# Moving the normalising passes of two layer norms from VectorE to GpSimd, with a new table of schedule settings

## The chip, the cores and the metric

The kernel runs on one core of a Trainium2 chip. A core has five engines that work side by side and wait for each other by semaphores: TensorE (PE, matmuls into the eight PSUM banks), VectorE (DVE), ScalarE (ACT), GpSimd (POOL) and SyncE (SP), which here issues nearly all DMAs. The metric is the device time of one execution in microseconds; of several runs the median is taken.

## The reference

From one input x of 2048 tokens by 512 features two branches are computed, and mixed by a gate of one number a token.

```python
def _layernorm(x, axis=-1, eps=1e-5):
    m = jnp.mean(x, axis=axis, keepdims=True)
    v = jnp.var(x, axis=axis, keepdims=True)
    return (x - m) / jnp.sqrt(v + eps)

# branch A: attention, 32 heads of 16
qkv = (x @ wqkv)                       # split into q, k, v by head
scores = einsum("bhqd,bhkd->bhqk", q, k) * (16 ** -0.5)
p = softmax(scores); o = einsum("bhqk,bhkd->bhqd", p, v)
a = o @ wo

# branch B: a mixer
h  = gelu(_layernorm(x) @ w1)          # 512 -> 512
hs = concat(four quarters of h, shifted by +1, -1, +2, -2 tokens) @ w2
x1 = x + hs
b  = x1 + gelu(_layernorm(x1) @ w3) @ w4   # 512 -> 1792 -> 512

g = sigmoid((x * gate_w).sum(-1))
out = g * a + (1 - g) * b
```

All inputs are bf16. Attention needs 32 x 2048 x 2048 exponentials; they are the largest piece of elementwise work.

## The kernel before

**Tiling.** Attention goes in 32 rounds: four chunks of 512 queries, four groups of eight heads, and the even or odd four heads of a group. A round has 64 score tiles, each 128 keys by 512 queries of one head: four heads on TensorE's four row groups, sixteen key tiles each. A score tile is one matmul (L1372, `qk_op`) and fills one PSUM bank. Altogether there are 2048.

**Two ways to the exponential.** Most score tiles go to ScalarE: `issue_act` (L1455) takes two or three tiles, and one exp instruction (L1467) turns their neighbouring banks into bf16 probabilities in SBUF (`prob`). For a three-tile instruction the knob `CAP3` has to allow it, for a two-tile one `CAP2` (L1783). The rest goes to VectorE: `issue_dve` (L1478) multiplies a score tile and adds an offset so that the result, rounded to a 16-bit integer, is the bit pattern of an approximate exponential (L1498). Two such tiles make a pair, and `close_pair` (L1518) derives three shifted copies of the pair by adding 32, 64 and 96 to the bits. A shift runs on VectorE (L1541) or on GpSimd (L1543); the knobs `GP2` and `GP3` set the share of either. The four versions together average the error out. A tile from ScalarE thus needs one value matmul (L1596, `take_pv`), a tile from VectorE four. Those write into one accumulator bank for a round, on TensorE's column groups.

**The end of a round.** `finish_round` (L1607) copies the accumulator to SBUF (L1617), sends the denominators through DRAM to be inverted and multiplied by the gate, and normalises on GpSimd (L1635); four small DMAs put the result into `oD`.

**The mixer.** The projections are matmuls of line L1002, cut into units of four matmuls on the four column groups; a few are done by rows (L1013). For a layer norm, `stats` (L1172 on) computes mean and variance of a 128-token tile on VectorE. `normalise` (L1180) handles a chunk of four tiles: variance plus epsilon (L1183) and its power of -0.5 (L1185) on GpSimd, minus mean times that (L1187) on VectorE, and then, for each tile, one pass over 128x512 (L1194) that multiplies by the one and adds the other. Its output is one of two `xn` buffers, which a DMA writes to DRAM (L1198) and frees; four transposing DMAs (L1204) read the chunk back into an `xnT` buffer, on which the matmuls with w1 or w3 depend. There are four chunks and two layer norms, so 32 passes. GELU runs over large blocks on ScalarE (L1214), with a table load before and another after (L1216).

**What sets the order.** The kernel's program is written out by a planner in Python while it is built (class `Sim`). Each engine has a list of jobs with a dependency list, a priority and an assumed duration (`hold`); `try_engine` (L330) lets a free engine take the ready job of the lowest priority number. TensorE's work is chosen by `pe_pick` (L1770): first score tiles for ScalarE and VectorE, then, in the time that it believes is left, units of projections and value matmuls. What it emits is the fixed order of each engine's instructions. Priorities and limits are knobs in a namespace `K`, from `BASE`, and a table `STEPS` overwrites some of them each time another `SEG = 8` score tiles have been issued:

```python
        if sim.tiles // SEG != stage[0]:
            for n in range(stage[0] + 1, sim.tiles // SEG + 1):
                K.__dict__.update(STEPS.get(n, {}))
```

Among them are `P1_PRIO` and `S_PRIO` (priorities of L1498 and L1541), `DVE_WAIT`, `DVE_STOP` and `DVE_ALONE` (how many tiles go to VectorE and when), `AHEAD` (how far score tiles may run into the next round), `MAXU` (most passes in one TensorE burst), `GATE` and `ROT`.

**The shared port.** `dve(..., port=True)` and every `gp(...)` job are ordered with one another: while one of them is believed to run, the planner starts no other, and each GpSimd instruction of that kind gets a wait for the last VectorE instruction of that kind before it (`in_port_order`, L315).

Of the kernel before, what the change touches and what calls it, by code (L numbers as in the profile page):

```python
# [452 lines left out]
def kernel(  # L453
# [14 lines left out]
    nc = tc.nc  # L468
# [66 lines left out]
        4: dict(P1_PRIO=0.136),  # L535
        5: dict(E_PRIO=0.1),
        6: dict(MAXU=3),
        7: dict(GP2=1, B_LOW=5),
        8: dict(E_PRIO=0.25, JOIN=1),
        9: dict(GP2=0.655),  # L540
        10: dict(GP2=1),
        11: dict(DVE_ALONE=-158),
        12: dict(LIMD=4),
        13: dict(AFIRST=0),
        14: dict(AFIRST=1),
        16: dict(DVE_STOP_L=16, PV_IDLE=0.117, PRESS=26),
        17: dict(IDLE_NS=864, B_LOW=8, ROT=0),
        18: dict(S_PRIO=0.38),
        19: dict(GP3=0.9),
        21: dict(GP3=0.8),  # L550
        22: dict(URG_L=18, PRESS=18),
        24: dict(GP3=0.9, URG_L=12, PRESS=26),
        25: dict(GP3=0.8, DVE_STOP=13, URG_L=18, PRESS=18),
        26: dict(AHEAD2=24, DUE_SH=32, GATE=3),
        27: dict(ROT=1),
        28: dict(SL0=-75, LIMA=2),
        29: dict(MAXG=2),
        30: dict(GP3=0.9, DUE_SH=-9),
        31: dict(GP3=0.8, DUE_SH=32),
        32: dict(GP3=0.967),  # L560
        33: dict(GP3=0.9, DUE_SH=-9),
        34: dict(PV_FULL=0.86, DUE_SH=16),
        35: dict(DVE_ALONE=2, ROT=0),
        36: dict(IDLE_NS=537, ROT=2, GATE=2),
        37: dict(P1_PRIO=0.55, ROWM=3),
        38: dict(SL1=-75, PV_FULL=0.813),
        39: dict(GP3=1, MAXG=1),
        40: dict(ROT=1),
        41: dict(S_PRIO=0.625, SL0=0, B_LOW=3, HOLE=2),
        42: dict(P1_PRIO=0.743, S_PRIO=0.3, GP3=0.8, DVE_STOP=4, DVE_STOP_L=14, URG=8, URG_L=12, DVE_ALONE=362, SL0=-75,  # L570
            IDLE_NS=374, AHEAD=12, PV_FULL=0.97, PV_IDLE=0.731, HOLE=3, MAXG=2, E_PRIO=2, AFIRST=2, ROWM=99, LIMA=4,
            JOIN=0),
        43: dict(ROT=2, AGE=6000),
        44: dict(MAXU=2, AGE=3000),
        45: dict(DVE_STOP_L=16, CAP2=5),
        46: dict(DVE_STOP_L=14, MAXU=3, CAP2=6, AGE=6000),
        47: dict(DVE_STOP=13, IDLE_NS=459, LIMA=3),
        48: dict(E_PRIO=0.4),
        49: dict(AT_SH=118),
        50: dict(ROT=3, ACC2=1),  # L580
        51: dict(GP3=1),
        52: dict(DVE_ALONE=-158, GATE=3, AGE=3000),
        53: dict(PV_FULL=0.813),
        54: dict(P1_PRIO=0.312, AHEAD=24),
        55: dict(BRES=2, MAXG=1),
        56: dict(URG=3, URG_L=18, SL1=-150, ROT=0),
        57: dict(URG_L=12, SL1=60, AGE=20000),
        58: dict(ROT=1),
        59: dict(SL1=130, B_LOW=2, PV_FULL=0.947),
        61: dict(LIMA=2),  # L590
        62: dict(SL1=-150),
        63: dict(P1_PRIO=0.55, DVE_STOP=8, URG=8, SL0=0, SL1=0, IDLE_NS=700, B_LOW=8, BRES=0, AHEAD=16, PV_FULL=0.86,
            PV_IDLE=0.117, ROT=0, DUE_SH=32, MAXG=2, GATE=2, E_PRIO=2, ACC2=0, LIMA=4),
        64: dict(URG=2, IDLE_NS=864, ROWM=3),
        65: dict(ROT=1),
        67: dict(E_PRIO=0.1),
        68: dict(URG=8, IDLE_NS=700, PV_FULL=0.947, CAP2=4, E_PRIO=2, ROWM=99, ACC2=1),
        69: dict(P1_PRIO=0.312),
        70: dict(LIMA=2),
        71: dict(GP3=0.8),  # L600
        74: dict(AHEAD=24, ROWM=3, LIMA=4),
        75: dict(URG=11),
        76: dict(DVE_WAIT=2),
        77: dict(URG=8, ROT=0, AGE=12000),
        79: dict(URG=11, DVE_WAIT=3, ROT=2, AGE=20000),
        80: dict(DVE_WAIT=2, ROT=1),
        81: dict(GP3=0.967),
        82: dict(URG=8),
        83: dict(P1_PRIO=0.279),
        84: dict(P1_PRIO=0.136, S_PRIO=0.38, GP3=1, URG=11, IDLE_NS=537, DVE_WAIT=3, AHEAD=3, PV_IDLE=0.5, ROT=0,  # L610
            AT_SH=34, CAP2=6, AGE=12000, ROWM=99, LIMA=3),
        85: dict(ACC2=0),
        86: dict(DVE_STOP_L=7, ROT=1),
        87: dict(DVE_STOP_L=14, ROT=0, ACC2=1),
        88: dict(AHEAD=9),
        89: dict(MAXU=9),
        90: dict(AGE=6000),
        91: dict(LIMA=2),
        93: dict(ROT=2),
        94: dict(ROT=0),  # L620
        95: dict(URG=2),
        96: dict(MAXU=2, JOIN=1),
        97: dict(MAXU=9, JOIN=0),
        98: dict(P1_PRIO=0.55, DVE_WAIT=4, PV_FULL=0.86),
        99: dict(LIMA=4),
        100: dict(URG=8, AT_SH=118),
# [1399 lines left out]
```

## Time and profile before

| | |
|---|---|
| Median of 3 runs | 744.62 us (744.61 to 744.85) |
| The profiled execution, in all | 744.89 us |
| Its span, first to last instruction | 742.9 us |
| TensorE clock granted | 1.000 |
| TensorE (PE) busy | 732.1 us, 99% |
| ScalarE (ACT) busy | 729.8 us, 98% |
| VectorE (DVE) busy | 678.8 us, 91% |
| GpSimd (POOL) busy | 479.0 us, 64% |
| DMA traffic | 34.60 MB, 47 GB/s on average |

The profile is of one execution. Busy time is time in which an engine has at least one instruction under way; two that overlap are counted once, but the mean duration of a group counts each in full, so 744 exps of 1.1 us fit into 685 us. Rows of groups read: line, engine, operation, output and input, shapes, count; then busy time in us and the mean in ns; then the idle time of the engine before these instructions and what ended it. Rows in order of time begin with start and duration in us. Rows of waits name who waited for whom, the time in all, how often, and the longest. PEld is the loading of weights into TensorE.

### The profile page before, as it was taken

Reading aid. Unit: us, or ns where it says so; the run is one execution under the profiler, and the core shown is the slowest. Engines: PE = TensorE matmul, PEld = TensorE weight load, DVE = VectorE, ACT = ScalarE, POOL = GpSimd, SP = SyncE. Lnnn points to the kernel's source line nnn. Section 1 sums busy time; section 2 is a strip of 40 time slices with the busy share of each in tenths; the row PEclk is TensorE's granted clock in tenths of the full one; section 3 lists DMA queues with packets and bytes.
Section 4 is the critical chain, followed back from the end, with each engine's and each line's share of the span. In section 5 each row is a group of like instructions: output and inputs, shape, how many; then the busy total and the mean of one; then the engine's idle time right before and its main releaser. Section 6 shows DMA issues by size and latency. Waiting matters only on the chain.

```text
span 742.9 us, 23801 instructions
## 1 busy us (share of the span) xinstructions
PE 732.1 (99%) x9550; PEld 212.8 (29%) x9550; DVE 678.8 (91%) x1407; ACT 729.8 (98%) x767; POOL 479.0 (64%) x478
## 2 busy tenths in 40 slices
PE   9999999999999999999999999999999999999997
PEld 5443232232222222222322222222222232222222
DVE  5899999999999999898998988999999997999995
ACT  7999999999999999999999999999999999999996
POOL 2247657788776757678557776667777767564441
PEclk9999999999999999999999999999999999999999
DMA  9520234022102132124100110002100000011001
GB/s 199 157 58 5 67 85 91 20 48 67 56 20 63 42 78 55 50 80 95 31 18 14 30 46 15 26 22 48 24 24 18 22 20 20 21 28 24 22 11 43
DMA packets 67094, 34.60 MB, mean 47 GB/s; under 512 B 46748, under 2 KB 62380, under 8 KB 66984
## 3 DMA queue, kind: packets, MB, share of 16 engines
q1 hardware_dynamic: 66040, 32.56, 17.6%
q8 instruction: 74, 1.21, 0.7%
q10 hardware_dynamic: 944, 0.52, 0.2%
q14 instruction: 36, 0.29, 0.1%
HBM read 17.40 MB, written 6.81 MB: 33 GB/s over the span
## 4 chain that ended last, share of the span: by engine, by line
PE 82%; ACT 13%; DVE 3%; issue 2%; ACTq 0%; DVEq 0%
PE banks L1596 29%; PE banks L1372 28%; PE banks L1002 24%; ACT prob L1467 10%; ACT hB L1214 2%; DVE prob L1541 1%; DVE prob L1498 1%; PE banks L981 0%; PE banks L1033 0%; ACT L1214 0%; ACT hT L1214 0%; ACT L1216 0%; PE banks L1127 0%; DVE accsb L1973 0%; DVE accsb L1976 0%
## 5 line engine op out<-in xcount | busy, mean ns | idle before, releaser
L1467 ACT ACTIVATE prob<-banks 128x1024 bf16<-128x1024 f32 (+1 forms) x744 | 685.3, 1146 | 1.1 <-PE banks L1002 0.8
L1543 POOL TENSOR_SCALAR prob<-prob 128x1024 uint16<-128x1024 uint16 x416 | 426.9, 1048 | 218.8 <-DVE prob L1541 97.0
L1498 DVE TENSOR_SCALAR prob<-banks 128x512 uint16<-128x512 f32 x553 | 367.1, 684 | 37.1 <-PE banks L1372 31.9
L1596 PE MATMUL banks<-prob,V 128*17 128x512 bf16 (+1 forms) x3713 | 313.5, 381 | 0.3
L1372 PE MATMUL banks<-q,kT 32*128 32x512 bf16 x2048 | 277.8, 384 | 3.6 <-ACT prob L1467 1.6
L1541 DVE TENSOR_SCALAR prob<-prob 128x1024 uint16<-128x1024 uint16 x418 | 158.4, 431 | 2.9 <-PE banks L1596 0.9
L1372 PEld LDWEIGHTS <-kT 32*128 32x128 bf16 x2048 | 69.9, 91 | 305.6 <-ACT prob L1467 282.0
L1596 PEld LDWEIGHTS <-V 128*17 128x17 bf16 (+1 forms) x3713 | 70.3, 88 | 116.3 <-issue 97.1
L1002 PE MATMUL banks<-xnT,w 128*32 128x512 bf16 x1152 | 96.5, 383 | 0.0
L1002 PE MATMUL banks<-w,hT 128*32 128x512 bf16 x692 | 59.7, 383 | 0.0
L1002 PEld LDWEIGHTS <-w 128*32 128x32 bf16 x1936 | 42.6, 95 | 50.3 <-issue 29.3
L1635 POOL TENSOR_TENSOR oT<-accsb,bcs 128x512 bf16<-128x512 f32 x31 | 39.5, 1275 | 26.1 <-DVE prob L1541 15.8
L1002 PE MATMUL banks<-w,w 128*32 128x256 bf16 (+1 forms) x784 | 41.0, 308 | 0.5 <-DVE prob L1498 0.4
L1002 PE MATMUL banks<-w,hB 128*32 128x512 bf16 x448 | 36.2, 382 | 0.4 <-ACT hB L1214 0.4
L1013 PE MATMUL banks<-wo,oD 32*128 32x512 bf16 x64 | 24.2, 384 | 0.0
L1617 DVE COPY accsb<-banks 128x512 f32<-128x512 f32 x31 | 21.2, 683 | 1.9 <-PE banks L1596 1.4
L1174 DVE BATCH_NORM_STATS2 st<-x_sb 128x6 f32<-128x512 bf16 x32 | 21.4, 678 | 0.0
L1002 PEld LDWEIGHTS <-hT 128*32 128x32 bf16 x692 | 14.7, 95 | 20.5 <-issue 14.2
L1268 DVE CAST hB<-banks 128x512 bf16<-128x512 f32 x28 | 18.9, 682 | 1.0 <-PE banks L1002 0.9
L1268 DVE CAST hT<-banks 128x512 bf16<-128x512 f32 x28 | 19.1, 682 | 0.7 <-PE banks L1002 0.5
L1002 PE MATMUL banks<-wo,oD 128*32 128x512 bf16 x176 | 19.5, 383 | 0.0
L1214 ACT ACTIVATE hT<-hT 128x7168 bf16<-128x7168 bf16 (+1 forms) x3 | 19.4, 6454 | 0.0
(94 smaller groups left out, 258.9 us busy)
## 6 DMA issues: line engine op xcount, KB each, us to landing
bcs<-rr SPq DMA_DIRECT2D x124, 64.0 KB, 2.0
xn_dram<-xn SPq DMA_DIRECT2D x32, 128.0 KB, 1.9
w<-in_B_w_dram SPq DMA_DIRECT2D x5, 512.0 KB
oD<-oT SPq DMA_DIRECT2D x124, 16.0 KB, 1.8
w<-in_B_w_dram SPq DMA_DIRECT2D x4, 448.0 KB
out_dram<-ot SPq DMA_DIRECT2D x14, 128.0 KB, 1.7
x_sb<-in_A_x_dram SPq DMA_DIRECT2D x3, 512.0 KB
w<-in_A_wqkv_dram SPq DMA_DIRECT2D x2, 256.0 KB
```

The costliest lines, as they stand in the source:

```text
L1002: units.append([Op("col", j, lambda j=j, lf=lf, rf=rf, n0=n0, n1=n1, st=st, sp=sp: nc.tensor.matmul(get()[32 * j:32 * j + 32, n0:n1], lhsT ...
L1013: o = Op("row", i, lambda: nc.tensor.matmul(get(), lhsT=lf(0, P)[rows], rhs=rf()[rows], start=False, stop=True, tile_position=(32 * i, 0), ...
L1174: a = dve(600, deps, lambda: nc.vector.bn_stats(out=sb.slot[:], in_=x_sb[:, t, :]), prio=6, at=at, acq=[sb])
L1214: g = nc.scalar.activation(out=ap, in_=ap, func=ACT.Gelu_apprx_tanh)
L1268: pre.append(evac(g, PSUM_NS, lambda ps, m=m: nc.vector.tensor_copy(out=h2()[:, m, :], in_=ps[:])))
L1372: o = Op("row", i, lambda: nc.tensor.matmul(dst(), lhsT=kT[G][32 * i:32 * i + 32, kt * P:(kt + 1) * P], rhs=qbuf[G, c].slot[32 * i:32 * i ...
L1467: job = act(hold, ops, lambda: nc.scalar.activation(out=prob[:, pb.cut(), :].bitcast(BF16), in_=unit()[:, rb.cut(), :], func=ACT.Exp, scal ...
L1498: return nc.vector.tensor_scalar(out=prob[:, b0.cut() if w == 2 else b0.bufs[h0].slot, :], in0=unit()[:, rb.cut() if w == 2 else rb.bufs[0 ...
L1541: return nc.vector.tensor_scalar(out=cut(k), in0=cut(0), scalar1=float(SHIFT * k), scalar2=None, op0=ALU.add)
L1543: return nc.gpsimd.tensor_scalar(out=cut(k), in0=cut(0 if both else 2), scalar1=1.0, scalar2=float(SHIFT * (k if both else 1)), op0=ALU.mu ...
L1596: return nc.tensor.matmul(one(accs[r])[32 * i:32 * i + n, :], lhsT=lhs(n), rhs=rhs(), start=st and not edge, stop=True, tile_position=(0, ...
L1635: n = gp(1250, d3, lambda: nc.gpsimd.tensor_tensor(out=ob.slot[:], in0=ab.slot[:], in1=bb.slot[:], op=ALU.mult), acq=[ob], frees=[ab, bb], ...
```

## The change

The pass of L1194 is created as a GpSimd job in place of a VectorE job, with an assumed duration of 592 ns for 323, and so on the GpSimd queue and in its port order:

```diff
             xb = Buf("xn", 1)
-            g = dve(323, [m], lambda t=t, xb=xb: nc.vector.tensor_scalar(
+            g = gp(592, [m], lambda t=t, xb=xb: nc.gpsimd.tensor_scalar(
                 out=xb.slot[:], in0=x_sb[:, t, :], scalar1=rs[which][:, t:t + 1], scalar2=nm[which][:, t:t + 1],
-                op0=ALU.mult, op1=ALU.add), prio=0.35, acq=[xb], port=True)
+                op0=ALU.mult, op1=ALU.add), prio=0.35, acq=[xb])
             last.append(g)
```

All of `STEPS` is replaced by another table, of which this is the beginning; the code that reads it is the same, and so is `BASE`:

```diff
     STEPS = {
-        0: dict(S_PRIO=0.3, DVE_STOP_L=7, SL0=0, IDLE_NS=374, AHEAD=16, AT_SH=69, AFIRST=1, AGE=20000),
-        1: dict(SL0=45, B_LOW=5, DVE_WAIT=1, AHEAD=9),
-        2: dict(AHEAD=7, MAXU=4, ACC2=1),
-        3: dict(SL0=0, B_LOW=3, DVE_WAIT=3, AHEAD=16, MAXU=9, ACC2=0),
...
+        0: dict(GP2=1, DVE_STOP=13, URG_L=18, SL0=60, MAXU=2, E_PRIO=0.25),
+        1: dict(P1_PRIO=0.55, URG_L=12, HOLE=0),
+        2: dict(AGE=20000),
+        3: dict(GP3=1, AT_SH=118),
+        4: dict(P1_PRIO=0.414, GP3=0.967, DVE_ALONE=-158, SL0=45, DVE_WAIT=2, AHEAD=16, AHEAD2=24, PV_FULL=0.86, MAXU=9,
+            AT_SH=34, HOLE=7, CAP3=5, GATE=4, E_PRIO=2, AGE=9000, ROWM=3),
...
```

Because the order is planned as a whole, a different table gives a different order on every engine, and other numbers of two-tile and three-tile exps, of score tiles on VectorE and of shifts on GpSimd. Counted in the built programs:

| instructions | before | after |
|---|---|---|
| exps over two tiles, three tiles, one tile (L1467) | 739, 5, 0 | 687, 42, 1 |
| score tiles on ScalarE, on VectorE | 1493, 555 | 1501, 547 |
| shifts of a pair on VectorE (L1541), on GpSimd (L1543) | 415, 416 | 444, 375 |
| normalising passes on VectorE, on GpSimd (L1194) | 32, 0 | 0, 32 |
| value matmuls (L1596) | 3713 | 3689 |
| DMAs issued by SyncE | equal | equal |

More of the change, by code (lines that the diff above doesn't have):

```diff
@@ L542 @@
[L542 to L568, printed above, removed]
@@ L614 @@
[L614 to L626, printed above, removed]
-        101: dict(P1_PRIO=0.414, AT_SH=0, ACC2=0),
-        102: dict(AFIRST=1),
```

387 lines of the change are left out of this document (194 added, 193 removed).

## The prediction

> **What bounds the kernel now.** I read the engine totals first, then ScalarE's own instructions in order of time, then the waits, and last the chain of work, which shows how TensorE and ScalarE hand over to each other.
>
> ```profile
> span 742.9 us, 23801 instructions
> PE 732.1 (99%) x9550; PEld 212.8 (29%) x9550; DVE 678.8 (91%) x1407; ACT 729.8 (98%) x767; POOL 479.0 (64%) x478
> 8.74 50.69 ACT L1467 ACTIVATE prob<-banks 128x1024 bf16<-128x1024 f32 x55
> ...
> 59.41 93.79 ACT L1467 ACTIVATE prob<-banks 128x1024 bf16<-128x1024 f32 x102
> 153.22 1.28 ACT L1214 ACT_TABLE_LOAD   x1
> ...
> 162.97 137.76 ACT L1467 ACTIVATE prob<-banks 128x1024 bf16<-128x1024 f32 x150
> 301.52 43.19 ACT L1467 ACTIVATE prob<-banks 128x1024 bf16<-128x1024 f32 x47 [0.79 <-PE banks L1002]
> 344.73 1.28 ACT L1214 ACT_TABLE_LOAD   x1
> ...
> 359.68 243.05 ACT L1467 ACTIVATE prob<-banks 128x1024 bf16<-128x1024 f32 x263
> 602.75 1.28 ACT L1214 ACT_TABLE_LOAD   x1
> ...
> 617.71 116.97 ACT L1467 ACTIVATE prob<-banks 128x1024 bf16<-128x1024 f32 x127
> 738.35 0.69 ACT L1992 ACTIVATE ot<-banks,omg 128x512 bf16<-128x512 f32 x1 [3.67 <-PE banks L1989]
> ```
>
> ScalarE runs without a gap from 8.74 us to 734.7 us, but for 0.79 us before 301.52. Its six stretches of softmax exponentials (L1467, "exps" below) are 50.69+93.79+137.76+43.19+243.05+116.97 = 685.45 us for 744 instructions. Between them lie three GELU blocks: 153.22 to 162.97 (9.75 us), 344.73 to 359.68 (14.95) and 602.75 to 617.71 (14.96). Ahead are 8.74 us, behind 742.9 - 734.68 = 8.2 us. That makes up the span. TensorE's 99% is not the same kind of number: who waits for whom must be asked.
>
> ```profile
> PEld L1372 <- ACT prob L1467: 282.0, 641, 1.0
> POOL prob L1543 <- DVE prob L1541: 97.0, 53, 8.6
> DVE prob L1498 <- PE banks L1372: 31.9, 89, 1.3
> 303.54 0.45 PE banks L1372 x4
> 303.98 0.54 PE banks L1596 x8
> 304.52 0.33 PE banks L1372 x3
> 304.85 0.59 PE banks L1596 x8
> ...
> 307.57 0.76 PE banks L1002 x12
> 308.33 0.32 PE banks L1372 x3
> ```
>
> The weight loads of the score matmuls (L1372) waited 641 times for an exp: TensorE gets its banks back from ScalarE. The chain shows the beat: a burst of scores 0.33 us, then eight other matmuls, which are two passes over the four column groups, 0.54 us: 0.87 us. Twelve, three passes, take 0.76 us, so a pass is 0.22 us and a change between bursts 0.54 - 2x0.22 = 0.10 us. VectorE has 64 us idle in the span and GpSimd 264 us.
>
> What one exp costs in the beat is read from the first and last starts in two stretches:
>
> ```profile
> L1467 ACT ACTIVATE prob<-banks x24: 1020/1162/1277, 118.3 to 139.1; 128x1024 bf16<-128x1024 f32 x24
> L1467 ACT ACTIVATE prob<-banks x7: 1168/1582/1657, 427.5 to 434.2; 128x1536 bf16<-128x1536 f32 x4, 128x1024 bf16<-128x1024 f32 x3
> L1467 ACT ACTIVATE prob<-banks 128x1024 bf16<-128x1024 f32 x739 | 679.8, 1143 | 1.1 <-PE banks L1002 0.8
> L1467 ACT ACTIVATE prob<-banks 128x1536 bf16<-128x1536 f32 x5 | 8.0, 1593 | 0.0
> ```
>
> The first row: 23 steps in 20.8 us, 0.904 us for an exp over two score tiles. The second: three wide and three narrow exps in 6.7 us, 2.233 a pair, so an exp over three tiles takes 1.329, and a tile more costs 0.425. (The durations of 1143 and 1593 ns overlap; they are not the pitch.) All 744 at these prices are 739x0.904 + 5x1.329 = 674.7 us. The stretches with their hole are 686.2; the six last exps drain some 0.24 us each, 1.4 together; the rest, 10.1 us, is waiting in small pieces. So ScalarE is the bound, with 10 us of slack in it at most.
>
> **The change, part by part.** Counts of the changed kernel are from its built program; durations are of the rows quoted.
>
> *The exps.* The new table of settings makes 687 two-tile exps of 739, 42 three-tile ones of 5, and one over a single tile (priced 0.904 - 0.425 = 0.479). That is 1501 score tiles on ScalarE for 1493, in 730 instructions for 744. The sum: -52x0.904 + 37x1.329 + 0.479 = -47.0 + 49.2 + 0.5 = **+2.6 us**, all on the path. Eight tiles are 8x0.425 = 3.4 us, and fourteen instructions saved give back 14x(0.904 - 0.850) = 0.8.
>
> The Trainium skill, "ScalarE: Activation LUTs", section "What ACT_TABLE_LOAD costs", gives another price for the step: 186 ns + 0.833 ns an element, less about 93 ns of overlap. By it the steps would be estimated at 0.946 and 1.373 us and the sum at +2.1; the trace's 0.904 is lower than that, and I keep the trace's.
>
> *The normalising passes.*
>
> ```profile
> L1194 DVE TENSOR_SCALAR xn<-x_sb,rs,nm 128x512 bf16<-128x512 bf16 x32 | 13.1, 433 | 1.3 <-DMA xn_dram<-xn 1.2
> L1543 POOL TENSOR_SCALAR prob<-prob 128x1024 uint16<-128x1024 uint16 x416 | 426.9, 1048 | 218.8 <-DVE prob L1541 97.0 <-PE banks L1596 38.2 <-PE banks L1372 24.8
> L1635 POOL TENSOR_TENSOR oT<-accsb,bcs 128x512 bf16<-128x512 f32 x31 | 39.5, 1275 | 26.1 <-DVE prob L1541 15.8 <-DMA bcs<-rr 3.6 <-DVE xn L1194 2.7
> L1708 POOL MEMSET oD<- 128x512 bf16 x1 | 0.5, 525 | 0.0
> L1498 DVE TENSOR_SCALAR prob<-banks 128x512 uint16<-128x512 f32 x553 | 367.1, 684 | 37.1 <-PE banks L1372 31.9 <-issue 0.2 <-PE banks L1596 0.2
> L1541 DVE TENSOR_SCALAR prob<-prob 128x1024 uint16<-128x1024 uint16 x418 | 158.4, 431 | 2.9 <-PE banks L1596 0.9 <-ACT prob L1467 0.6
> ```
>
> 32 passes of 0.433 us leave VectorE, 13.9 us. On GpSimd no such pass is shown: the 512-wide memset is 0.525 us, the two-input 512-wide product 1.275, the same kind of operation at double width 1.048. It lies nearest to half of the last plus its fixed part; I take 0.62, so 20 us, with ends of 17 and 41. GpSimd at the same time does 375 shifts (L1543) for 416: -41x1.048 = -43. It ends between 453 and 477 us busy, under the 479 it has: covered, and 0 on the path. Without this cover a chunk of four passes would cost up to 4x1.275 = 5.1 us once it is on the path.
>
> *VectorE's other work.* 547 score tiles (L1498) for 555: 547 single ones for 551, and none of two double ones, about -4x0.684 - 2x1.22 = -5.2. The shifts (L1541) rise by 29, +29x0.431 = +12.5. With the passes gone: -6.6 of 679 us. VectorE is not the bound, so 0.
>
> *TensorE.* Counting four matmuls on different column or row groups as one pass: column passes 1834 to 1819.5, row passes 709 to 724, changes between bursts 1404 to 1412: +0.5x0.22 + 8x0.10 = +0.9 us, on an estimated 2543x0.22 + 1404x0.10 = 700 us. ScalarE's exps and GELU blocks are 674.7 + 39.7 = 714. So TensorE has some 2% to spare, and +0.9 is hidden as long as single bursts are. A burst of three passes beside a two-tile exp (0.33 + 0.76 against 0.904) is over by 0.18: those rise from 98 to 109, at most +2.0. Bursts of four rise from 8 to 29, but 20 of the 29 stand beside a three-tile exp with 1.329 us of cover. I take 0 and keep +2.0 as the end.
>
> *Queues.* SP issues as many DMAs as before, the 32 writes of xn and 32 transposing reads among them, with the writes in another place:
>
> ```profile
> xn_dram<-xn SPq DMA_DIRECT2D x32, 128.0 KB, 1.9
> xnT<-xn_dram SPq DMA_TRANSPOSE x32, 2.7
> 300.66 0.41 DVE L1194 TENSOR_SCALAR xn<-x_sb,rs,nm 128x512 bf16<-128x512 bf16 x1 [0.42 <-DMA xn_dram<-xn]
> ```
>
> There are two xn buffers. The third pass of a chunk waits until the first's write has landed (1.9 us after issue); on VectorE that held up everything behind it for 0.42 us here. On GpSimd the same wait would hold shifts, and with them the value matmuls of their tiles, which are late next; its 97 us of waiting for VectorE's shifts alone are larger than 16 waits of 1.9. In the programs the last transposing read of a chunk precedes its first matmul by at least 11 exps, 10 us, where it was 6 before, against 2.7 us to landing. So 0.
>
> Head and tail: the same instructions lie before the first exp and, but for the width of the last one, behind it: 0.
>
> Sum: +2.6. The profiled execution took 744.89 us in all, its span 742.9; 744.89 + 2.6 = 747.5. It lies 0.27 above the median of 744.62, so I expect a median of **747.3 us**, +0.35%. About 0.2%, 1.5 us, is what a measurement of this kernel can tell from no change.
>
> **Rivals.**
>
> *The waits shrink: faster.* VectorE has 6.6 us less to do and its hold-ups by L1194 are gone, three-tile exps give bursts of four passes their cover, and the 10.1 us of small waits go to half: 747.3 - 5 = 742.3. The point from which it decides is 2.6 + 1.5 = 4.1 us of 10.1. For it speaks that the largest single hole (0.79 us before 301.52, behind an L1002 burst) comes right where VectorE stood 0.42 us at an xn pass. Against it: the other holes are too short for the waits to list, VectorE itself waits 31.9 us for scores, so relieving it need not bring scores sooner, and three-pass bursts beside two-tile exps become more. 0.12.
>
> *Gain and loss cancel:* the waits give back between 1.2 and 4: within 1.5 us of 744.6. The order was made anew throughout, and I have no row for its waits. 0.14.
>
> *GpSimd comes onto the path.* If a pass there is as slow as the product (1.275), or waits in line behind a shift (1.048), xn is written later and the first matmuls of a chunk hold up TensorE, which works in order. At the one hole of 0.79 us shown for each of eight chunks: +6.3, 753.6; at two or three chunks 749 to 750. The distances of 10 us and more speak against it. Within it, three-pass bursts that overshoot add up to 2.0: 749.3. Together 0.14.
>
> The Trainium skill speaks for that rival: "GPSIMD Engine Reference", section "4.1 Engine selection", sends elementwise work on a tile to VectorE and calls GpSimd about twice as slow with two inputs, though near line rate with one. An estimate by the 2.6 cycles an element of its section 3.1 is 1.1 us a pass; that lies inside the ends above, and no run here shows it yet.
>
> *The move doesn't do what it says:* the passes do leave VectorE in the built program, so no chance is kept for that.
>
> **How the numbers follow.** The forecast, 746.2 to 749.0, has 0.60; GpSimd or TensorE adding more 0.14; no measurable change 0.14; faster 0.12. So slower 0.74, same 0.14, faster 0.12. The range runs from 744.2, which leaves out the rival of shrunken waits but takes in most of the cancelling case, to 750.4, which is 747.3 + 2.0 and another hole of 0.79 with 0.3 to spare; about 2 in 10 stay outside.
>
> **What would show it.** Steps over two tiles of 0.904 and over three of 1.33; ScalarE without gaps from 8.7 us on, its stretches adding up to 688 or 689; xn on GpSimd at 0.6 us with GpSimd's busy time near 456 and VectorE's near 672; the rows of waits of L1002 for xnT empty. It is wrong if the stretches of exps are 685 or shorter (small waits gone), if xn passes come out above 1 us with holes on ScalarE before L1002 bursts, or if the tail behind the last exp is no longer 8.2 us.

## The result, and the profile after

The changed kernel takes 748.81 us (median; 748.21 to 750.36) and the kernel before, run beside it, 744.74 us (744.61 to 745.33). The ratio is 1.0050, with a 95% interval of 1.0031 to 1.0069: 4.1 us more, where 747.3 us and +2.6 were forecast. The profiled execution took 749.05 us in all, its span 747.2. In the profile of the changed kernel each line from the one of the exps on has a number 39 lower than before: exps L1428, score tiles on VectorE L1459, shifts L1502 (VectorE) and L1504 (GpSimd), scores L1333, value matmuls L1557, projections L963, passes L1155.

The page of the changed kernel (its span and engine totals), and ScalarE's instructions in order of time (start, duration, then what they are; in brackets the idle time ahead and who ended it):

```profile
span 747.2 us, 23772 instructions
PE 733.6 (98%) x9534; PEld 214.5 (29%) x9534; DVE 685.4 (92%) x1398; ACT 733.0 (98%) x753; POOL 463.3 (62%) x469
8.47 59.57 ACT L1428 ACTIVATE prob<-banks 128x1024 bf16<-128x1024 f32 x55
...
67.91 16.41 ACT L1428 ACTIVATE prob<-banks 128x1024 bf16<-128x1024 f32 x14
84.90 30.58 ACT L1428 ACTIVATE prob<-banks 128x1024 bf16<-128x1024 f32 x27 [0.58 <-PE banks L1333]
115.69 45.52 ACT L1428 ACTIVATE prob<-banks 128x1536 bf16<-128x1536 f32 x49 [0.21 <-PE banks L1333]
...
170.97 104.14 ACT L1428 ACTIVATE prob<-banks 128x1024 bf16<-128x1024 f32 x113
275.71 69.77 ACT L1428 ACTIVATE prob<-banks 128x1024 bf16<-128x1024 f32 x76 [0.59 <-POOL prob L1504]
...
360.45 232.91 ACT L1428 ACTIVATE prob<-banks 128x1024 bf16<-128x1024 f32 x254
...
608.33 115.76 ACT L1428 ACTIVATE prob<-banks 128x1024 bf16<-128x1024 f32 x126
724.32 14.35 ACT L1428 ACTIVATE prob<-banks 128x1024 bf16<-128x1024 f32 x16 [0.24 <-ACT prob L1428]
```

The nine stretches add up to 689.01 us for 730 exps, against 685.45 for 744. At the prices of the prediction (0.904, 1.329, 0.479) the exps of the changed kernel are 677.3 us against 674.7: +2.6. Four holes, all in brackets above, make 0.58 + 0.21 + 0.59 + 0.24 = 1.62 us, against one of 0.79. Stretches and holes, less the price and less the 1.4 us that the ends drain, are what ScalarE waited inside: 11.9 us, against 10.1. So the trace splits the 4.3 us by which the span grew into **+2.6 of more exponentials, +1.8 of more waiting**, 0.3 less ahead of the first exp (8.47 for 8.74) and 0.3 more behind the last (747.2 - 738.67 = 8.5 for 8.2), within rounding.

The three GELU blocks cut the span into four parts. In each, the time from the first exp to the last, less its exps at their prices and with the drains left in, is what ScalarE waited there: 2.5, 3.7, 3.6 and 1.7 us before, and 3.8, 3.7, 3.3 and 2.4 us after. So the added waiting lies ahead of the first GELU block, where half of the passes and all three-tile exps stand, and behind the last, where no pass stands; between the first and the second, where the other half of the passes stands, there is none.

Two of the four holes lie at normalising passes. Around the first, the trace of the changed kernel in order of time:

```profile
81.81 0.77 POOL L1155 TENSOR_SCALAR xn<-x_sb,rs,nm 128x512 bf16<-128x512 bf16 x1 [1.18 <-DMA xn_dram<-xn]
82.55 2.22 POOL L1504 TENSOR_SCALAR prob<-prob 128x1024 uint16<-128x1024 uint16 x2
82.82 2.23 DVE L1502 TENSOR_SCALAR prob<-prob 128x1024 uint16<-128x1024 uint16 x2
83.65 0.40 PE L1557 MATMUL banks<-prob,V 128*17 128x512 bf16 x4 [0.99 <-POOL prob L1504]
```

GpSimd stands 1.18 us at a pass, until the DMA that writes an earlier one has freed an `xn` buffer. The shift behind it comes late, TensorE waits 0.99 us at a value matmul for that shift, with scores queued behind it, and ScalarE then stands 0.58 us for scores (84.90 above). Ahead of 275.71 it is GpSimd again: two passes of 0.77 us start there after 1.93 us of waiting for VectorE, and the exp waits for a shift queued behind them. The other waits are as finely spread as before.

Groups of the changed kernel, form by form (busy us, mean ns of one, then idle time of the engine ahead of them); the group of all its shifts on VectorE as the page has it; and the durations of those shifts before, then after, as minimum, median and maximum:

```profile
L1428 ACT ACTIVATE prob<-banks 128x1024 bf16<-128x1024 f32 x687 | 640.6, 1148 | 1.7 <-POOL prob L1504 0.6 <-PE banks L1333 0.6 <-ACT prob L1428 0.2
L1428 ACT ACTIVATE prob<-banks 128x1536 bf16<-128x1536 f32 x42 | 66.1, 1573 | 0.4 <-PE banks L1333 0.2
L1155 POOL TENSOR_SCALAR xn<-x_sb,rs,nm 128x512 bf16<-128x512 bf16 x32 | 24.9, 783 | 23.0 <-DVE nm L1148 8.7 <-DVE prob L1502 5.5 <-DVE x_sb L1217 3.1
L1504 POOL TENSOR_SCALAR prob<-prob 128x1024 uint16<-128x1024 uint16 x375 | 385.2, 1045 | 216.6 <-DVE prob L1502 129.2 <-ACT prob L1428 26.9 <-PE banks L1557 23.8
L1459 DVE TENSOR_SCALAR prob<-banks 128x512 uint16<-128x512 f32 x547 | 361.9, 682 | 27.9 <-PE banks L1333 23.7 <-POOL prob L1504 0.3
```

```profile
L1502 DVE TENSOR_SCALAR prob<-prob 128x1024 uint16<-128x1024 uint16 x447 | 183.8, 453 | 7.6 <-PE banks L1557 3.4
```

```profile
L1541 DVE TENSOR_SCALAR prob<-prob x418: 283/419/1347, 12.3 to 733.4; 128x1024 uint16<-128x1024 uint16 x139, 128x512 uint16<-128x512 uint16 x1
```

```profile
L1502 DVE TENSOR_SCALAR prob<-prob x447: 284/419/1493, 11.6 to 737.0; 128x1024 uint16<-128x1024 uint16 x148, 128x512 uint16<-128x512 uint16 x1
L1155 POOL TENSOR_SCALAR xn<-x_sb,rs,nm x32: 762/768/1008, 34.4 to 278.9; 128x512 bf16<-128x512 bf16 x32
```

VectorE lost 13.1 us of passes and about 5.2 us of score tiles, and yet its busy time rose by 6.6 us (678.8 to 685.4), because its shifts went from 158.4 to 183.8 us: 29 more of them, and a mean of 453 ns for 431 at the same median. A pass on GpSimd takes 0.768 us at the median.

### The profile page after: what moved, and what is told of

Its sections match the earlier page's. It is cut to its first block, busy times and chain, and to the rows that moved or that the text cites. A ratio compares the mean times of both kernels' runs of the same rounds, so it can differ in the third digit from the quotient of the medians.

```text
span 747.2 us, 23772 instructions
## 1 busy us (share of the span) xinstructions
PE 733.6 (98%) x9534; PEld 214.5 (29%) x9534; DVE 685.4 (92%) x1398; ACT 733.0 (98%) x753; POOL 463.3 (62%) x469
## 4 chain that ended last, share of the span: by engine, by line
PE 66%; ACT 20%; DVE 5%; issue 5%; POOL 2%; DMA 1%; SPq 0%; POOLq 0%; ACTq 0%; DVEq 0%
PE banks L1333 23%; PE banks L1557 22%; PE banks L963 20%; ACT prob L1428 17%; DVE prob L1459 2%; DVE prob L1502 2%; POOL prob L1504 1%; ACT hB L1175 1%; ACT hT L1175 1%; POOL xn L1155 0%; PE banks L942 0%; ACT L1175 0%; ACT L1177 0%; DMA xn_dram<-xn 0%; SPq L1592 0%
## 5 line engine op out<-in xcount | busy, mean ns | idle before, releaser
L1428 ACT ACTIVATE prob<-banks 128x1024 bf16<-128x1024 f32 (+1 forms) x730 | 688.5, 1172 | 2.1 <-PE banks L1333 0.8
L1504 POOL TENSOR_SCALAR prob<-prob 128x1024 uint16<-128x1024 uint16 x375 | 385.2, 1045 | 216.6 <-DVE prob L1502 129.2
L1459 DVE TENSOR_SCALAR prob<-banks 128x512 uint16<-128x512 f32 x547 | 361.9, 682 | 27.9 <-PE banks L1333 23.7
L1557 PE MATMUL banks<-prob,V 128*17 128x512 bf16 (+1 forms) x3689 | 317.7, 382 | 1.4 <-POOL prob L1504 1.2
L1333 PE MATMUL banks<-q,kT 32*128 32x512 bf16 x2048 | 282.0, 385 | 5.3 <-ACT prob L1428 3.0
L1502 DVE TENSOR_SCALAR prob<-prob 128x1024 uint16<-128x1024 uint16 x447 | 183.8, 453 | 7.6 <-PE banks L1557 3.4
L1333 PEld LDWEIGHTS <-kT 32*128 32x128 bf16 x2048 | 71.0, 91 | 306.0 <-ACT prob L1428 277.1
L1557 PEld LDWEIGHTS <-V 128*17 128x17 bf16 (+1 forms) x3689 | 72.5, 89 | 116.9 <-issue 97.8
L963 PE MATMUL banks<-xnT,w 128*32 128x512 bf16 x1152 | 99.6, 383 | 0.4 <-DVE prob L1459 0.3
L963 PE MATMUL banks<-w,hT 128*32 128x512 bf16 x688 | 60.5, 384 | 0.1
L1596 POOL TENSOR_TENSOR oT<-accsb,bcs 128x512 bf16<-128x512 f32 x31 | 39.7, 1280 | 28.8 <-DVE prob L1502 19.3
L963 PEld LDWEIGHTS <-w 128*32 128x32 bf16 x1936 | 42.7, 95 | 50.7 <-issue 29.9
L1155 POOL TENSOR_SCALAR xn<-x_sb,rs,nm 128x512 bf16<-128x512 bf16 x32 | 24.9, 783 | 23.0 <-DVE nm L1148 8.7
L963 PE MATMUL banks<-w,w 128*32 128x256 bf16 (+1 forms) x784 | 38.9, 308 | 0.2 <-DVE prob L1459 0.2
L963 PE MATMUL banks<-w,hB 128*32 128x512 bf16 x448 | 37.9, 382 | 0.3 <-ACT hB L1175 0.3
L974 PE MATMUL banks<-wo,oD 32*128 32x512 bf16 x80 | 28.5, 384 | 0.0
L963 PE MATMUL banks<-w,wq 128*32 128x512 bf16 x256 | 20.5, 382 | 0.0
L963 PEld LDWEIGHTS <-hT 128*32 128x32 bf16 x688 | 14.1, 95 | 20.5 <-issue 16.2
```

Source lines behind the costliest of these rows:

```text
L963: units.append([Op("col", j, lambda j=j, lf=lf, rf=rf, n0=n0, n1=n1, st=st, sp=sp: nc.tensor.matmul(get()[32 * j:32 * j + 32, n0:n1], lhsT ...
L974: o = Op("row", i, lambda: nc.tensor.matmul(get(), lhsT=lf(0, P)[rows], rhs=rf()[rows], start=False, stop=True, tile_position=(32 * i, 0), ...
L1155: g = gp(592, [m], lambda t=t, xb=xb: nc.gpsimd.tensor_scalar(out=xb.slot[:], in0=x_sb[:, t, :], scalar1=rs[which][:, t:t + 1], scalar2=nm ...
L1333: o = Op("row", i, lambda: nc.tensor.matmul(dst(), lhsT=kT[G][32 * i:32 * i + 32, kt * P:(kt + 1) * P], rhs=qbuf[G, c].slot[32 * i:32 * i ...
L1428: job = act(hold, ops, lambda: nc.scalar.activation(out=prob[:, pb.cut(), :].bitcast(BF16), in_=unit()[:, rb.cut(), :], func=ACT.Exp, scal ...
L1459: return nc.vector.tensor_scalar(out=prob[:, b0.cut() if w == 2 else b0.bufs[h0].slot, :], in0=unit()[:, rb.cut() if w == 2 else rb.bufs[0 ...
```

## The experiments

Twelve kernels ran, beside the kernel before and partly beside one another. The table holds them all. "Stretches", "holes" and "waits" come from ScalarE's instructions in order of time, worked out as above (waits = stretches + holes - exps at their prices - 1.4); they are of one profiled execution each, the ratio is of repeated runs.

| kernel | order, passes on | ratio to before (95%) | span us | stretches + holes | exps at their price | waits |
|---|---|---|---|---|---|---|
| before | old, VectorE | 1 | 742.9 | 685.45 + 0.79 | 674.7 | 10.1 |
| after | new, GpSimd | 1.0050 (1.0031 to 1.0069) | 747.2 | 689.01 + 1.62 | 677.3 | 11.9 |
| old_order_gp | old, GpSimd | 1.0049 (1.0035 to 1.0063) | 747.4 | 687.08 + 4.08 | 674.7 | 15.1 |
| new_order_dve | new, VectorE | 1.0076 (1.0063 to 1.0089) | 749.0 | 689.43 + 1.88 | 677.3 | 12.6 |
| new_order_dve_4buf | new, VectorE | 1.0053 (1.0039 to 1.0067) | 746.9 | 689.09 + 0.67 | 677.3 | 11.1 |
| new_order_4buf | new, GpSimd | 1.0040 (1.0027 to 1.0053) | 747.7 | 689.14 + 1.99 | 677.3 | 12.4 |
| old_order_4buf | old, VectorE | 0.9987 (0.9976 to 0.9997) | 742.1 | 685.48 + 0 | 674.7 | 9.4 |
| short_pass | new, GpSimd | 1.0037 (1.0024 to 1.0049) | 745.4 | 688.51 + 0.63 | 677.3 | 10.4 |
| double_pass | new, GpSimd | 1.0336 (1.0321 to 1.0351) | 767.5 | 690.92 + 19.68 | 677.3 | 31.9 |
| drop8 | new, GpSimd | 1.0034 (1.0024 to 1.0045) | 745.7 | 687.10 + 2.00 | 673.9 | 13.8 |
| short_drop8 | new, GpSimd | 1.0031 (1.0019 to 1.0044) | 744.8 | 686.75 + 1.69 | 673.9 | 13.1 |
| act_probe | old, VectorE | 1.0047 (1.0034 to 1.0061) | 748.5 | 699.61 + 1.40 (stretches overlap the probes) | with 5.8 of probes | |
| hold700 | planned anew | 1.0418 (1.0402 to 1.0435) | 775.1 | 696.56 + 21.02 | 684.6 | |
| hold560 | planned anew | 1.0557 (1.0534 to 1.0579) | 783.7 | 703.23 + 24.54 | 689.5 | |

### One part of the change at a time

**new_order_dve** keeps the changed kernel's order, but the pass itself is issued on VectorE, where the plan has a GpSimd instruction:

```diff
-            g = gp(592, [m], lambda t=t, xb=xb: nc.gpsimd.tensor_scalar(
+            g = gp(592, [m], lambda t=t, xb=xb: nc.vector.tensor_scalar(
...
-                op0=ALU.mult, op1=ALU.add), prio=0.35, acq=[xb])
+                op0=ALU.mult, op1=ALU.add), prio=0.35, acq=[xb], name="xn")
```

In the port order it counts as a VectorE instruction.

> The order of the changed kernel on every engine, but each normalising pass is issued to VectorE in its place. Theory A, late GpSimd: of the 4.3 us by which the span grew, 2.7 are the longer exps and 1.6 come from passes that hold GpSimd longer than the order assumed (0.78 us for 0.59) and so stall VectorE's shifts and GpSimd's own; then this kernel has the exps' 2.7 and about 10 us of waits again: 747.3 us, between 746.5 and 747.8, and the holes on ScalarE near 83, 114 and 274 us are gone. Theory B, the new order itself makes the waits: it stays at 748.8 within 0.5.

It was slower than the changed kernel, 1.0076. It too has a hole at the chunk shown above, in the trace of new_order_dve:

```profile
82.89 0.41 DVE L1155 TENSOR_SCALAR xn<-x_sb,rs,nm 128x512 bf16<-128x512 bf16 x1 [0.75 <-DMA xn_dram<-xn]
...
83.96 0.39 PE L1333 MATMUL banks<-q,kT 32*128 32x512 bf16 x1 [0.83 <-DVE prob L1459]
...
85.48 5.97 ACT L1428 ACTIVATE prob<-banks 128x1536 bf16<-128x1536 f32 x5 [1.18 <-PE banks L1333]
```

Now VectorE stands at the pass for a free `xn` buffer, and behind the pass on VectorE stand score tiles whose banks TensorE needs: 0.83 us on TensorE, 1.18 us on ScalarE, twice the hole that GpSimd's wait left there. The two kernels have the same exps in the same order, so each exp's start can be set against the same exp's: new_order_dve is 1.3 us later at exp 53 (64.1 us in the changed kernel), 2.7 at this hole, and 1.2 again at exp 97, because the changed kernel's own holes at 84.90 and 115.69 are missing here. So this hole costs what those two cost; of the 1.8 us by which the profiled run is longer, 0.6 lie ahead of the first exp (9.09 for 8.47), the rest in small waits elsewhere. So the new order with fast passes isn't cheaper; the two `xn` buffers are tried below.

**old_order_gp** is the other half: the old order and table, the pass issued on GpSimd.

```diff
-            g = dve(323, [m], lambda t=t, xb=xb: nc.vector.tensor_scalar(
+            g = dve(323, [m], lambda t=t, xb=xb: nc.gpsimd.tensor_scalar(
...
-                op0=ALU.mult, op1=ALU.add), prio=0.35, acq=[xb], port=True)
+                op0=ALU.mult, op1=ALU.add), prio=0.35, acq=[xb], port=True, name="xn")
```

> The order of the kernel before on every engine, but each normalising pass is issued to GpSimd in its place. Exps as before: 739 over two tiles, 5 over three. Theory A: the same hold-ups appear here, +1 to +3 us: 746 to 748. Theory B: the engine of the pass is free, 744.7 within 0.5, or a little less where VectorE held up something.

It took 1.0049, with exactly the exps of before: all of it is waiting, 15.1 us for 10.1, and 4.08 us of that in holes. The largest, in the trace of old_order_gp:

```profile
279.04 0.25 DVE L1624 RECIPROCAL pk<-pk 128x16 f32<-128x16 f32 x1 [1.87 <-DMA pk<-den]
279.90 0.39 PE L1372 MATMUL banks<-q,kT 32*128 32x512 bf16 x1 [1.41 <-DVE prob L1498]
282.19 1.02 ACT L1467 ACTIVATE prob<-banks 128x1024 bf16<-128x1024 f32 x1 [2.32 <-PE banks L1372]
```

VectorE waits 1.87 us for denominators to come back from DRAM; score tiles stand behind that, and ScalarE ends up 2.32 us short. SP issued that read late, behind writes of an `oT` that GpSimd normalised after two passes; that this is why is read from the order of the queues and was not tried by itself. What comes of it is in the same trace, TensorE's busy time and granted clock (PEclk) microsecond by microsecond:

```profile
core 0: us, PE busy (x), PEclk, DMA share, GB/s
278.00:279.00 1.00, 0.49 (x6) 1.00 0.21 65
279.00:280.00 1.00, 0.10 (x1) 1.00 0.23 75
281.00:282.00 1.00, 1.00 (x11) 0.50 0.00 0
285.00:286.00 1.00, 1.00 (x19) 1.00 0.00 0
```

TensorE has little to do for two microseconds, and from 280.9 to 284.3 us its granted clock is 0.50; twelve matmuls of L1002 then take 1.13 us (at 280.49) where twelve took 0.83 (at 272.00). The kernel before and the changed kernel have no such drop up to the last exp. Set exp by exp against the kernel before, this run falls back by 3.5 us between 278 and 286 us, the hole and the slow clock together, and by little elsewhere. So most of what the move cost here comes from one place. The mean granted clock was 0.996 to 0.998 in all five runs of this kernel, against 0.998 to 1.000 for the kernel before beside it, which fits a drop in each; only one run was profiled.

**What follows.** The engine alone, in an order planned for VectorE's pass of 323 ns, costs as much as the whole change (1.0049 and 1.0050), and the order alone costs it too, 1.0053 once it has buffers enough (below). The two don't add. Had the forecast been of the move alone, its "0 on the path" would have been wrong by 3.6 us.

### Is GpSimd's time covered?

**short_pass** lets the passes from the third on work on 300 of their 512 columns, so that one takes what the planner assumed. Normalising the other columns is left out.

```diff
-                out=xb.slot[:], in0=x_sb[:, t, :], ...
+                out=xb.slot[:, 0:512 if which == 0 and t < 2 else 300], in0=x_sb[:, t, 0:512 if which == 0 and t < 2 else 300], ...
```

> The changed kernel, but from the third pass on the pass covers 300 of 512 columns (the normalisation of the rest is left out and stale columns are written), so a pass lasts about what the order assumed (estimate 0.78 x 300/512 plus its fixed part, 0.5 to 0.6 us). Theory A: half or more of the extra waits go, 747.3 to 748.2, and VectorE's shifts above 0.6 us become fewer than 30. Theory B: 748.8 within 0.5.

**double_pass** issues each pass twice, 32 x 0.768 = 24.6 us more for an engine that is idle for 284 us of the span.

```diff
+            def twice(t=t, xb=xb):
+                for _ in range(2):
+                    g = nc.gpsimd.tensor_scalar(out=xb.slot[:], in0=x_sb[:, t, :], ...)
+                return g
+            g = gp(592, [m], twice, prio=0.35, acq=[xb])
```

> The changed kernel with every pass issued twice on GpSimd, 25 us more on GpSimd, which has over 250 us idle. Theory A: the hold-ups grow by more than they were, +2 to +6 us: 751 to 755. Theory B: 748.8 to 749.5, since GpSimd is off the path.

The passes of short_pass, and ScalarE in it up to the first GELU block, where the changed kernel had another hole at 115.69; then of double_pass the passes, two of its holes, and ScalarE behind the last pass:

```profile
L1155 POOL TENSOR_SCALAR xn<-x_sb,rs,nm x32: 584/592/848, 34.0 to 276.7; 128x300 bf16<-128x300 bf16 x30, 128x512 bf16<-128x512 bf16 x2
84.02 76.21 ACT L1428 ACTIVATE prob<-banks 128x1024 bf16<-128x1024 f32 x76 [0.40 <-PE banks L1333]
```

```profile
L1157 POOL TENSOR_SCALAR xn<-x_sb,rs,nm x64: 762/768/1438, 34.3 to 299.4; 128x512 bf16<-128x512 bf16 x64
78.34 1.45 ACT L1431 ACTIVATE prob<-banks 128x1536 bf16<-128x1536 f32 x1 [3.69 <-PE banks L1336]
...
223.81 1.02 ACT L1431 ACTIVATE prob<-banks 128x1024 bf16<-128x1024 f32 x1 [2.79 <-POOL prob L1507]
...
305.13 60.60 ACT L1431 ACTIVATE prob<-banks 128x1024 bf16<-128x1024 f32 x66 [0.20 <-PE banks L1336]
...
380.70 232.91 ACT L1431 ACTIVATE prob<-banks 128x1024 bf16<-128x1024 f32 x254
```

Twice the passes cost 1.0336 - 1.0050 = 2.9% or 21 us: of 24.6 us of extra work on an engine with 284 us to spare, the end moved by more than four fifths, far above the 2 to 6 us that were expected. The holes add up to 19.7 us, and all but the 0.24 ahead of the last stretch lie between 43 and 305 us, where the passes are; from there on ScalarE runs as in the changed kernel (254 exps in 232.91 us in both). Each pass stands in a fixed queue ahead of shifts that are due, and so idle time elsewhere in the span is no cover for it. The 21 us are not queueing alone, though: in this trace the granted TensorE clock is 0.50 for 6.8 us from 73.4 us and for 3.4 us from 223.6, beside two gaps in which TensorE had next to nothing to do (73.0 to 75.9 and 219.6 to 222.8). It worked some 7.7 us at half the clock, an estimated 3.9 us lost, which a single pass does not cost: the changed kernel's clock is 1.00 there. In the other direction, short_pass, with 30 x 0.176 = 5 us less GpSimd work, brought waits back from 11.9 to 10.4 us and the ratio from 1.0050 to 1.0037, about 1 us, and VectorE's shifts above 0.6 us from 30 to 25; the two intervals overlap, so that the size is an estimate. The pass's price beyond the plan's 592 ns is thus worth some 1 to 1.5 us of the 4.1.

### The two buffers

Four `xn` buffers in place of two, in the same order of instructions: for the first layer norm they are slices of `hB`, for the second the two of before and the two of `ot`.

```diff
+    hB4 = hB[:].rearrange("p (n d) -> p n d", d=D)
+    xn4 = lambda which, t: hB4[:, t % 4, :] if which == 0 else (sim_xn + sim_ot)[t % 4][:]
...
-                out=xb.slot[:], in0=x_sb[:, t, :], ...
+                out=xn4(which, t), in0=x_sb[:, t, :], ...
...
-                out=xn_dram[which, t * P:(t + 1) * P, :], in_=xb.slot[:]), frees=[xb]))
+                out=xn_dram[which, t * P:(t + 1) * P, :], in_=xn4(which, t)), frees=[xb]))
```

This was done to the changed kernel, to the kernel before, and to new_order_dve.

> The changed kernel with four xn buffers where two were, so that no pass waits for the write of the one before the last; the order is the same, passes on GpSimd at 0.78 us. If the waits for the buffer make the hold-ups, the hole near 83 us goes and the time falls by 0.5 to 1.5 us from 748.8: 747.3 to 748.3. If it is the length of the pass alone: 748.8 within 0.4.

> The kernel before, passes on VectorE, with four xn buffers. VectorE waited twice for a buffer, 1.2 us in all, once just before the largest hole on ScalarE (0.79 us at 301.5). If that wait makes the hole: -0.5 to -1 us, 744.0 to 744.5. If the hole comes from TensorE's burst ahead of it: no change within 0.3.

> The order of the changed kernel with the passes on VectorE, 1.0076 of the kernel before, and now four xn buffers. If its excess over the changed kernel is VectorE standing still for a buffer, with the releases of banks behind it (0.75 us ahead of the hole of 1.3 us near 83 us), it falls to 748.8 or below, a ratio of 1.005 or less. If it is VectorE's 13 us more work in an order that has no place for them: 1.007 to 1.008.

In new_order_4buf the ratio 1.0040 lies inside the interval of the changed kernel, and its waits are 12.4 us for 11.9, so no gain from the buffers is shown here; the hole near 84 went, and another of twice its size came, again behind shifts on GpSimd:

```profile
113.36 0.59 PE L1560 MATMUL banks<-prob,V 128*17 128x512 bf16 x4 [0.78 <-POOL prob L1507]
114.38 1.45 ACT L1431 ACTIVATE prob<-banks 128x1536 bf16<-128x1536 f32 x1 [1.30 <-PE banks L1336]
```

In old_order_4buf the pass no longer waits (it had 0.42 us ahead of it before), the hole of 0.79 us at 301.52 is gone, and ScalarE runs from one GELU block to the next without one:

```profile
162.97 180.89 ACT L1470 ACTIVATE prob<-banks 128x1024 bf16<-128x1024 f32 x197
299.81 0.41 DVE L1197 TENSOR_SCALAR ot<-x_sb,rs,nm 128x512 bf16<-128x512 bf16 x1
```

Its ratio is 0.9987 (0.9976 to 0.9997), about 1 us, which is the hole and a little (exp by exp, 0.7 of the 0.9 us by which the last exp comes earlier arise at that hole): the fastest kernel of this study, though by less than the 0.2% that counted as measurable at the outset. new_order_dve_4buf falls from 1.0076 to 1.0053, the intervals overlapping at their ends. The hole at 85.48 is gone; exp by exp, 1.1 of the 2.1 us between the two profiled runs arise there, and 0.6 ahead of the first exp, where the buffers have no part. So about half of the difference is shown to be the wait for a buffer. With that away the new order costs 0.5% with passes on VectorE (1.0053) and 0.4% with passes on GpSimd (1.0040); the intervals overlap. Against the old order with the same four buffers (0.9987) it costs 0.7% with passes on VectorE. **In the new order the cost is there with either engine**; in the old order the move alone made as much (old_order_gp). How much of the changed kernel's waits is the engine's and how much the order's, no run separates; the +2.6 us of exponentials are the order's.

### Does ScalarE's work set the time?

**act_probe** adds to the kernel before 62 exponentials of a single column, one behind each twelfth exp.

```diff
+            if extra:
+                nc.scalar.activation(out=mb[:].bitcast(F32), in_=zero[:, 0:1], func=ACT.Exp)
```

> The kernel before with one activation of a single column behind every twelfth exp, 62 in all at 0.11 us each by the row behind the GELU blocks: 6.8 us more on ScalarE and nothing elsewhere. If ScalarE is the bound: +5.5 to +7, about 751.5. If TensorE sets the beat and ScalarE only looks full: below +2.

**drop8** takes eight of the changed kernel's three-tile exps back to the price of two tiles: each fifth of the first forty works on 341 of 512 columns a tile, and a third of its exponentials is left out.

```diff
+        n_exp[0] += w == 3
+        cols = 341 if w == 3 and n_exp[0] % 5 == 0 and n_exp[0] <= 40 else 512
```

> The changed kernel, but 8 of its 42 three-tile exps (every fifth) cover 341 of 512 columns of each tile, which is the work of two tiles (a third of their exponentials is left out): 8 x 0.427 = 3.4 us off ScalarE, the surplus of eight tiles over the kernel before. If ScalarE is the bound, the time falls by 3.4 with an end of 2.4: 745.4 to 746.4. If TensorE sets the beat where three-tile exps stand (bursts of four passes), it falls by less than 1: above 747.8.

**short_drop8** has the edits of short_pass and of drop8 together.

> The changed kernel with both: passes over 300 columns from the third on, and 8 three-tile exps cut to the work of two tiles (normalisation and exponentials left out as there). Alone they brought the ratio from 1.005 to 1.0037 and 1.0034. If the two are separate costs they add up: 1.002, 746.5 us. If late passes and ScalarE's surplus are waited out at the same places, 1.003 or above.

Two probes of act_probe with the twelve exps between them, then the three-tile exps of drop8, short and full ones:

```profile
513.92 0.29 ACT L1474 ACTIVATE mb<-zero 128x1 f32<-128x1 bf16 x1
514.02 11.20 ACT L1472 ACTIVATE prob<-banks 128x1024 bf16<-128x1024 f32 x12
524.97 0.33 ACT L1474 ACTIVATE mb<-zero 128x1 f32<-128x1 bf16 x1
```

```profile
L1431 ACT ACTIVATE prob<-banks 128x1023 bf16<-128x1023 f32 x8 | 8.8, 1095 | 0.1
L1431 ACT ACTIVATE prob<-banks 128x1536 bf16<-128x1536 f32 x34 | 50.6, 1487 | 1.4 <-PE banks L1333 0.8
```

A probe takes 0.10 us of the beat (513.92 to 514.02), 62 of them 5.8 us, and the kernel grew by 0.34% to 0.61%, 2.5 to 4.5 us. drop8 saves 8 x 0.425 = 3.4 us on ScalarE, and the ratio fell from 1.0050 to 1.0034, 1.2 us, the span by 1.5. So ScalarE's work is on the path, but not all of it: 0.43 to 0.78 of what is added, about 0.4 of what is taken away, the latter between two intervals that overlap. The rest goes into the waits, which grow from 11.9 to 13.8 us in drop8: the 34 full three-tile exps now have 1.4 us of idle time ahead of them, most of it for scores, where all 42 had 0.4. They lie between 21 and 116 us. Of the 3.4 us taken off, 2.3 come back as waits ahead of the first GELU block (3.8 us there become 6.1), so there TensorE must be about as late as ScalarE; that is argued from these waits, not measured.

short_drop8 came to 1.0031, hardly below either edit alone. The gains of both would have made 1.002, which its interval (1.0019 to 1.0044) still takes in, so the ratio alone doesn't show that they fail to add up. The trace of short_drop8 shows where a part is lost:

```profile
80.20 1.17 POOL L1155 TENSOR_SCALAR xn<-x_sb,rs,nm 128x300 bf16<-128x300 bf16 x2 [2.31 <-DMA xn_dram<-xn]
83.84 2.54 ACT L1431 ACTIVATE prob<-banks 128x1024 bf16<-128x1024 f32 x2 [1.19 <-PE banks L1333]
```

Exp by exp, it is 1.1 us ahead of short_pass at exp 64 (76.6 us there) and 0.2 ahead at this hole: GpSimd, sooner at the pass, waits 2.31 us for the write of an `xn` buffer, where it waited 1.18 in the changed kernel. In the end it is 0.6 ahead.

### The table and its one trajectory

**hold700** and **hold560** change one figure of the plan, the pass's assumed duration, and let the new table plan the order again.

```diff
-            g = gp(592, [m], lambda t=t, xb=xb: nc.gpsimd.tensor_scalar(
+            g = gp(700, [m], lambda t=t, xb=xb: nc.gpsimd.tensor_scalar(
```

> The changed kernel with the pass assumed at 700 ns in the plan for 592, which is nearer to the 768 it takes; all of the order is planned anew, with 695 exps over two tiles, 42 over three and one over one: 684.7 us at 0.904, 1.331 and 0.478, 7.3 more than the changed kernel's 677.4. If ScalarE's sum sets the time: 754 to 756. If it is paid in part, as with the shortened exps (a third): 751. If the better assumption for the pass takes the waits out: below 751.

> As before with 560 ns: 701 exps over two tiles and 42 over three, 689.6 us, 12.2 more than the changed kernel's. If ScalarE's sum sets the time: 759 to 761; paid to a third: 753; the pass is later against its plan than in the changed kernel, 0 to +1.

Neither is near. Their exps cost 7.3 and 12.2 us more than the changed kernel's, and the kernels take 27 and 38 us more (3.7% and 5.1%); the difference is holes. Of hold700:

```profile
473.99 5.60 ACT L1428 ACTIVATE prob<-banks 128x1024 bf16<-128x1024 f32 x6 [4.06 <-PE banks L1557]
L1428 ACT ACTIVATE prob<-banks 128x1024 bf16<-128x1024 f32 x695 | 651.5, 1127 | 21.2 <-PE banks L1557 10.3 <-PE banks L1333 8.0 <-issue 1.4
```

The hole of 4.06 us lies 190 us behind the last pass, so no pass stands in it. The settings come due by count of score tiles, and meet another state of the queues here than in the order they were found with; that this makes the holes is argued. A pass priced more truly can't be tried with this table alone: 700 is nearer to the measured 768 than 592 is, and the order came out worse.

## Why the prediction was right or wrong

- **Direction and range: right.** Slower by 0.50%, inside 744.2 to 750.4; the forecast of 747.3 was 1.5 us too low, and the time fell at the upper edge of the 746.2 to 749.0 that it gave the likeliest case. That it came so near is in part luck: the term that it forecast was worth less on the path than it said, and waits that it put at nothing made up for it.
- **The exps, +2.6: right as a count.** The stretches came to 689.0 us (688 or 689 forecast). The steps held too: in the rows below seven exps, four wide and three narrow, again take three pairs in 6.7 us, 2.233 a pair; 27 two-tile steps in 24.6 us are 0.911, with the small waits in them. "All on the path" was too much: act_probe and drop8 put 0.4 to 0.8 of such work on the path, which makes 1 to 2 us of the 2.6.

```profile
L1428 ACT ACTIVATE prob<-banks x7: 1178/1592/1667, 55.1 to 61.8; 128x1536 bf16<-128x1536 f32 x4, 128x1024 bf16<-128x1024 f32 x3
L1428 ACT ACTIVATE prob<-banks x28: 1116/1172/1241, 369.5 to 394.1; 128x1024 bf16<-128x1024 f32 x28
```

- **The pass, 0.62 us: low, inside its ends.** It took 0.768 at the median. The estimate of 1.1 us from the Trainium skill, "GPSIMD Engine Reference", section 3.1, was too high by 0.33: that section gives the 2.6 cycles an element for an operation with two inputs, and the pass has one. Section 4.1 of that page calls GpSimd about twice as slow with two inputs and near line rate with one; the trace agrees that one input is cheaper, 0.768 us for the pass against 1.275 for the two-input product of the same width (which reads f32).
- **"Covered, and 0 on the path": the step that failed, as far as the runs show.** GpSimd's busy time did fall, to 463 us (453 to 477 forecast), but busy time is a sum over the span and says nothing of where a pass stands. Two holes open behind GpSimd's passes or buffer waits, 1.2 us together; double_pass made 21 us out of 24.6, some of it by TensorE's slower clock; old_order_gp cost 3.6 us with nothing else changed, most of it at one place. How much of the changed kernel's 1.8 us of added waiting is the passes' is known by short_pass alone, 1 to 1.5 us with overlapping intervals.
- **"97 us of waiting for VectorE's shifts alone are larger than 16 waits of 1.9": wrong in kind.** The wait for the buffer came, 1.18 us on GpSimd ahead of 81.81, and showed on ScalarE as 0.58. With four buffers that hole went, and a like one opened at 114.38.
- **VectorE, -6.6: came out +6.6.** The counts were right; a shift's mean was not. Two shifts that run beside two of GpSimd's took 2.23 us (82.82 above), where one alone takes 0.42. The Trainium skill, "SBUF — State Buffer", section "Who interferes with whom", says that a VectorE instruction in a two-port mode and GpSimd lock each other out for a whole instruction, first come first served; the trace agrees in that shifts above 0.6 us (12 before, 30 after) all ran beside a GpSimd instruction, and it shows the blocked time as busy time of VectorE; in which mode the shifts run, no run here shows. On the path it is not seen apart from the rest.
- **TensorE, 0 with an end of +2.0; head and tail, 0.** Head and tail moved by -0.3 and +0.3. TensorE's own share was not isolated; that ScalarE waits longer for scores once exps are shortened in drop8 says that its cover at 21 to 116 us is thinner than the 2% over the whole span.
- **The rivals.** "The waits shrink" and "gain and loss cancel" did not come: waits are 11.9 us, not 5 to 9. "GpSimd comes onto the path" came in part, with its 749 to 750 for two or three chunks nearer to the 748.8 than mine, but by another way than its price: not first matmuls of a chunk waiting for `xnT`, for which no row of waits names a DMA, but value matmuls waiting for shifts behind a pass.

**What stays open.** Of 4.1 us, 1 to 2 are more work on ScalarE, 1 to 1.5 the pass beyond its assumed 592 ns. With both edits (short_drop8) the new order is still 0.31% slower, 2.3 us; its one large hole, 1.19 us, starts from a wait for an `xn` buffer, and the rest of its waits are too short for the list. As the edits meet each other's waits, no sum of single causes is shown.

## What to carry to other kernels

In a program whose order is fixed on every engine, an engine's idle time over the span is no cover: ask of each moved instruction what is queued behind it, who waits for that, and double the instruction to see, with an eye on the granted clock, which the doubled kernel may lose and the single one not. A change of order costs or gains by itself, so test the order with the old engine and the engine with the old order; here each cost as much as both together. Look for a short write-out wait at the head of a queue before moving work to another engine: two more buffers gave the old kernel 0.13%, with nothing moved, though in the new order with passes on GpSimd they gave nothing that shows.

## What the runs showed of the hardware

A one-input GpSimd pass with two operands of one number a partition took 0.768 us over 512 bf16 columns and 0.592 us over 300: 0.83 ns a column and an estimated 0.34 us beside it, so that a shorter pass saves less than its share. VectorE's shift, 0.42 us alone, took up to 1.49 us (1.35 before) when GpSimd was at work, and the profile counts all of it as busy: VectorE's busy time rose by 6.6 us where work of 18 us was taken from it and some 12 us added. In old_order_gp the granted TensorE clock stood at 0.50 for 3.4 us from 1 us after a wait of 1.41 us at a score matmul; in the changed kernel, with a wait of 0.99 us at a value matmul, it stayed at 1.00. And a probe of one column costs ScalarE 0.10 us between two exps, although its own row shows about 0.3.
